# Later times in an instruction planner for attention weight parts, transposed keys and loaded queries

## The chip, the cores and the metric

The kernel runs on one core of a Trainium2 chip. The core has a matrix engine (TensorE, in the profile PE, with PEld for its weight loads), a vector engine (VectorE, DVE), a scalar engine (ScalarE, ACT), GpSimd (POOL) and SyncE (SP), which here issues DMAs. Each engine works through its own list of instructions in the order in which the program wrote them, and waits by semaphores for others. The metric is the device time of one execution in microseconds, smaller is better.

## The reference

Block-sparse attention for 4 batches of 8 heads, 768 positions and head size 64 is followed by a bilinear feed-forward network on the 3072 rows of its output:

```python
scores = scale * np.matmul(q, k.transpose(0, 1, 3, 2))
mask = np.abs(blk_i - blk_j) <= 1              # blocks of 32 positions, 24 of them
mask = mask | (blk_i == 0) | (blk_j == 0) | (blk_i == n_blocks - 1) | (blk_j == n_blocks - 1)
# and three sampled key blocks for each query block
attn = softmax(np.where(mask, scores, -1000000000.0))
x = (attn @ v).transpose(0, 2, 1, 3).reshape(3072, 512)
return ((x @ w_a) * (x @ w_b)) @ w_out         # 512 -> 1536 -> 512
```

## The kernel before

All products run in float16 with each operand split in a high and a low part, so that most products are made three times.

**Attention** works in units: one unit is one block of 32 query rows of one batch, 24 blocks in 4 batches, 96 units. A sparse unit (88 of them) gathers eight key blocks (POOL copies from the transposed keys `keysT` to `KG`) and eight value blocks (SP DMAs to `VG`); PE makes the scores `s` (L1024, L923); DVE takes the maximum `low` (L1039, L1042); ACT makes the exponentials `sm` (L1049); ACT or DVE write the high part of the weights and DVE the low part into a buffer `hl` (`in_parts`, L941, L944, L948); a DMA transpose turns `hl` into `pt` (L1074); PE multiplies `pt` with the values to `av` (L967); ACT and DVE split that into `xT` (L1233, L1236). The first and last block of each batch are dense: four pieces each, with their transposes at L1188. There are three buffers `hl` and three `pt`. The first eight units turn their weights on PE instead (L1101). In the text a unit is named by its number in the order of work, so `hl32` is the buffer contents of unit 32.

**Chunks.** Eight units make a chunk of 256 rows. For each chunk ACT issues the loads of its queries `q` in two halves (L691), reads them for a bound (L701), scales them (L706), DVE makes the low part (L708), and SP copies both to the other half of the partitions. **Feed-forward** takes a chunk's `xT` in twelve pieces: 24 matmuls `ab` (L1265), ACT and DVE make the product `a` and its parts `gh` and `gl` (L1282, L1285, L1294, L1297), six matmuls `o` (L1325 to L1327). A piece needs the whole chunk's `xT`. In the first 230 us DVE and ACT also turn the raw weights into parts (L768 to L816).

**The order** of every engine's list comes from a planner that runs when the program is built (`Plan`, L131). Each piece of work is a generator: it yields a `Way` (an engine, a duration in ns, what to issue), an `Event` it must wait for, or a number of ns by which it sleeps. The planner always issues the piece that can begin first by its own clock; ranks break ties and weigh on DVE and SP. A `Ring` gives out buffers: `take` waits until the one that is a ring's length back was freed, at the time its `fire` was given. For a DMA the planner reckons its own landing time (`issue`, L156). Times in the plan decide the order alone; on the chip the semaphores decide when an instruction starts. The names that matter here are `gone`, the event by which a buffer `hl` comes free (L1077, L1191), `done` and `k_ready` in `keys` (L524, L525), and the load in `queries` (L693).

Of the kernel before, what the change touches and what calls it, by code (L numbers as in the profile page):

```python
# [52 lines left out]

LATE_PT, LATE_VG, LATE_AV, LATE_G = 2500, 2500, 1500, 700
LATE_S = 1000
DMA_AHEAD = 1750
X_HIGH, X_UNITS = 600, 16

# [190 lines left out]
def kernel(  # L249
# [94 lines left out]
    k_ready = [Event(NG) for _ in range(B)]  # L344
# [143 lines left out]
    def keys(b, g):  # L488
        yield from gate(first_of[b] - GATE_KV)
        raw, freed = yield from raw_tile(b, g, 0)  # L490
        yield load_way(1000, lambda: nc.scalar.dma_start(raw, k[b, g]))
        if g + 1 < NG:
            plan.start(keys(b, g + 1), first_of[b] - LEAD_K)
        elif b > 0:
            plan.start(values(b, 0), first_of[b] - LEAD_V)
        t = raw.rearrange("p (t d) -> p t d", d=D)
        done = yield from take("ks", KS_BUFS)
        ks = work.tile([P, 2 * NT, P], F16, tag="ks", name=f"ks{b}_{g}", bufs=KS_BUFS)
        at = at_k + b * NG + g
        s = scale[:, at : at + 1]  # L500
        yield act(1020, lambda: nc.scalar.activation(
            ks[:, :, :D], t, AF.Abs, accum_out=bound[:, at : at + 1]
        ))
        end = yield from set_scale(slice(at, at + 1), FLOOR_QK)
        k_scale[b].fire(end)
        yield act(930, lambda: nc.scalar.activation(ks[:, :, :D], t, AF.Copy, scale=s))
        end = yield dve(1070, lambda: nc.vector.scalar_tensor_tensor(
            ks[:, :, D:], t, s, ks[:, :, :D], ALU.mult, ALU.subtract
        ))
        freed.fire(end)  # L510
        if b == 0:
            ends = Event(2)
            for h in range(2):
                plan.start(turn_keys(g, h, ks, ends, done), first_of[b] - LEAD_K, end)
            return
        if b == 1:
            yield w_freed
        if b >= 2:
            yield k_free[b - 2]
        end = yield sp(1700, 2200, lambda: nc.sync.dma_start_transpose(  # L520
            keysT[b % 2][:, 2 * g : 2 * g + 2, :].rearrange("p h (t s) -> p (h t) s", s=P),
            ks.rearrange("p t d -> p (t d)"),
        ))
        done.fire(end)  # L524
        k_ready[b].fire(end)  # L525

    def load_eye():
        end = yield load_way(100, lambda: nc.scalar.dma_start(eye, c_eye))
# [152 lines left out]
    def queries(cc):  # L681

        b, c = chunks[cc]
        u0 = order[b, c * PER]
        yield from gate(u0 - GATE_Q)
        freed = yield from take("rq", 1)
        t = work.tile([P, H, CH], F32, tag="rq", name=f"q{cc}", bufs=1)

        def load():
            for hs in (slice(0, H // 2), slice(H // 2, H)):  # L690
                nc.scalar.dma_start(t[:D, hs], q[b, c][:, hs])  # L691

        yield [Way("LOAD", 950, load, 1400, 1)]  # L693
        if cc + 1 < NC:
            b1, c1 = chunks[cc + 1]
            plan.start(queries(cc + 1), order[b1, c1 * PER] - LEAD_Q)
        at = at_q + cc
        q_used[cc] = yield from take("QT", QT_BUFS)
        QT[cc] = work.tile([P, 2, H, CH], F16, tag="QT", name=f"QT{cc}", bufs=QT_BUFS)
        high, low_ = QT[cc][:D, 0], QT[cc][:D, 1]  # L700
        yield act(2080, lambda: nc.scalar.activation(  # L701
            high, t[:D], AF.Abs, accum_out=bound[:D, at : at + 1]
        ))
        yield from set_scale(slice(at, at + 1), FLOOR_QK)
        s = scale[:D, at : at + 1]
        end = yield act(1890, lambda: nc.scalar.activation(high, t[:D], AF.Copy, scale=s))  # L706
        plan.start(turn_queries(cc, 0), u0 - LEAD_Q, end)
        end = yield dve(2350, lambda: nc.vector.scalar_tensor_tensor(  # L708
            low_, t[:D], s, high, ALU.mult, ALU.subtract
        ))  # L710
        freed.fire(end)
        plan.start(turn_queries(cc, 1), u0 - LEAD_Q, end)
        yield k_scale[b]

        def factor():

            for i in range(2):
                ps = slice(i * 64, (i + 1) * 64)
                nc.vector.tensor_scalar(
                    cq[ps, cc, :],  # L720
                    rscale[ps, at_k + b * NG : at_k + (b + 1) * NG].rearrange(
                        "p (a i) -> p a i", i=2
                    )[:, :, i],
                    rscale[ps, at : at + 1], float(D) ** -0.5, ALU.mult, ALU.mult,
                )

        end = yield dve(520, factor)
        q_ready[cc].fire(end)
# [278 lines left out]
    def attend(b, i):  # L1007
# [27 lines left out]
        t = yield pe(850, all_scores)  # L1035
# [35 lines left out]
        if n < TURNED:  # L1071
            yield from turn_weights(n, hl, pt, gone)
        else:
            t = yield sp(1300, 1500, lambda: nc.sync.dma_start_transpose(  # L1074
                pt, hl.rearrange("p a h k -> p (a h k)")
            ))
            gone.fire(t)  # L1077
            yield LATE_PT
        yield vg_ready[b, i, 0]
        yield from before(b, i)  # L1080
# [42 lines left out]
    def attend_quad(b, i, hq, ends):  # L1123
        n = order[b, i]
        cc = chunk_at[b, i // PER]
        kt = keysT[b % 2]
        at = n % LATE
        if hq > 0:
            yield quad_sent[b, i]
        reads, banks = [], []  # L1130
        for x in range(2):
            reads.append((yield from take("s", 2)))
            banks.append(psum.tile([P, HALF], F32, tag="s", name=f"s{n}_{hq}{x}", bufs=2))

        def half_scores(x):
            scores(
                banks[x], cc, i, hq, lambda h: kt[:, h, x * HALF : (x + 1) * HALF], True
            )

        for x in range(2):  # L1140
            t = yield pe(450, lambda x=x: half_scores(x))
        if hq == 0:
            quad_sent[b, i].fire(t - HOP)
        else:
            k_free[b].fire(t)
            next_unit(b, i, t - HOP)
        for x in range(2):
            yield dve(530, lambda x=x: nc.vector.tensor_reduce(
                low[:, at, hq, x : x + 1], banks[x], axis=mybir.AxisListType.X, op=ALU.max,
                negate=True,  # L1150
            ))
        m1 = low[:, at, hq, 0:1]
        yield dve(270, lambda: nc.vector.tensor_scalar(
            m1, m1, low[:, at, hq, 1:2], cq[:, cc, hq : hq + 1], ALU.min, ALU.mult
        ))
        sms, freed = [], []
        mine = yield from turn("sm", b, i, hq)
        for x in range(2):
            freed.append((yield from take("sm", SM_BUFS)))
            if x == 1:  # L1160
                mine.fire(0)
            sms.append(work.tile([P, HALF], F32, tag="sm", name=f"sm{n}_{hq}{x}", bufs=SM_BUFS))
            t = yield act(860, lambda x=x: nc.scalar.activation(
                sms[x], banks[x], AF.Exp, bias=m1, scale=cq[:, cc, hq : hq + 1],
                accum_out=den[:, at, hq, x : x + 1],
            ))
            reads[x].fire(t + LATE_S)
        d1 = den[:, at, hq, 0:1]
        d2 = den[:, at, hq, 1:2]
        yield dve(212, lambda: nc.vector.tensor_scalar(d1, d1, d2, EPS, ALU.add, ALU.add))  # L1170
        yield dve(150, lambda: nc.vector.tensor_scalar(
            d1, d1, float(2.0 ** -14), None, ALU.mult
        ))
        yield dve(160, lambda: nc.vector.reciprocal(d1, d1))
        mine = yield from turn("hl", b, i, hq)
        mine_pt = yield from turn("pt", b, i, hq)
        for x in range(2):
            gone = yield from take("hl", HL_BUFS)
            if x == 1:
                mine.fire(0)  # L1180
            hl = work.tile([P, 2, HALF], F16, tag="hl", name=f"hl{n}_{hq}{x}", bufs=HL_BUFS)
            t = yield from in_parts(sms[x], hl[:, 0], hl[:, 1], d1, HALF, False)
            freed[x].fire(t)
            kept = yield from take("pt", PT_BUFS)
            if x == 1:
                mine_pt.fire(0)
            pt = work.tile([P, 6, P], F16, tag="pt", name=f"pt{n}_{hq}{x}", bufs=PT_BUFS)
            t = yield sp(1100, 1130, lambda hl=hl, pt=pt: nc.sync.dma_start_transpose(  # L1188
                pt, hl.rearrange("p a k -> p (a k)")
            ))  # L1190
            gone.fire(t)  # L1191
            plan.start(all_values(b, i, hq, x, pt, kept), n, t + LATE_PT)

    def all_values(b, i, hq, x, pt, kept):
# [261 lines left out]
```

## Time and profile before

| | us |
|---|---|
| median of 3 runs | 874.8 |
| lowest and highest of them | 874.49, 878.71 |
| the profiled execution's own time | 871.27 |
| its span, from the first to the last instruction | 869.5 |
| PE busy in the span | 759.1 |
| DVE, ACT, POOL busy | 590.8, 501.3, 191.7 |

Busy time counts an instruction from its start to its end; waiting counts as idle. An instruction that waits holds back everything behind it on its engine. PE's ends are modelled, since matmuls overlap.

### The profile page before, as it was taken

How to read it: one execution, taken by the hardware profiler on the slowest of the kernel's cores; microseconds unless marked ns; L12 is line 12 of the kernel's file. 1: busy time of each engine (PE TensorE's matmuls, PEld its weight loads, DVE VectorE, ACT ScalarE, POOL GpSimd, SP SyncE). 2: the span in 40 equal slices, each digit the busy share in tenths (PEclk: the TensorE clock that was granted, in tenths of full speed). 3: DMA queues.
4: the chain of work that ended last, by engine and by line, in shares of the span. 5: the costliest groups of instructions: out<-in, count | busy, mean ns of one | idle time of the engine just before them, and what ended most of it. 6: DMA issues, size and time to landing. Idle time of an engine off the chain costs nothing.

```text
span 869.5 us, 24163 instructions
## 1 busy us (share of the span) xinstructions
PE 759.1 (87%) x9136; PEld 561.9 (65%) x9136; DVE 590.8 (68%) x1609; ACT 501.3 (58%) x1191; POOL 191.7 (22%) x428
## 2 busy tenths in 40 slices
PE   2246367599999979999999999999999999999998
PEld 1134245377767757766776667677777677777775
DVE  4979988999788666766576696766677776432222
ACT  6579787866766464774355586644656554332222
POOL 0743253200034232330032242200342310000000
PEclk9996689999999999999999999999999999999999
DMA  8766798795967479896586899767966766610000
GB/s 244 211 182 201 223 228 188 179 246 128 243 172 183 118 155 215 194 176 178 134 166 170 162 209 239 160 152 172 168 143 161 144 138 159 142 44 1 25 2 25
DMA packets 195151, 138.74 MB, mean 160 GB/s; under 512 B 138073, under 2 KB 162650, under 8 KB 195034
## 3 DMA queue, kind: packets, MB, share of 16 engines
q1 hardware_dynamic: 183104, 99.40, 52.3%
q10 hardware_dynamic: 11930, 37.79, 14.4%
q8 instruction: 72, 1.18, 0.6%
q14 instruction: 45, 0.37, 0.1%
HBM read 86.28 MB, written 12.58 MB: 114 GB/s over the span
## 4 chain that ended last, share of the span: by engine, by line
PE 47%; DVE 18%; DMA 18%; ACT 10%; issue 4%; SPq 2%; ACTq 1%; POOL 0%; POOLq 0%; DVEq 0%
PE ab L1265 25%; DMA pt<-hl 6%; PE av L967 5%; PE o L1325 5%; DMA q<-in_q_dram 5%; PE o L1327 4%; PE o L1326 4%; PE s L923 3%; DVE hl L948 2%; DMA VG<-vd 2%; DMA stage<-in_k_dram 2%; DVE QT L708 2%; DVE xT L1236 2%; ACT sm L1049 1%; ACT QT L706 1%
## 5 line engine op out<-in xcount | busy, mean ns | idle before, releaser
L1265 PE MATMUL ab<-xT,wab 128*128 128x256 f16 x3456 | 401.4, 273 | 6.0 <-DVE xT L1236 3.2
L1265 PEld LDWEIGHTS <-wab 128*128 128x128 f16 x3456 | 334.4, 98 | 68.5 <-issue 13.8
L1285 DVE SCALAR_TENSOR_TENSOR a<-a,to_g,ab 128x256 f32<-128x256 f32 x144 | 68.6, 477 | 104.8 <-ACT a L1282 103.7
L1282 ACT ACTIVATE a<-ab,w 128x256 f32<-128x256 f32 x144 | 67.3, 467 | 112.0 <-PE ab L1265 109.6
L1049 ACT ACTIVATE sm<-s,low,cq 128x256 f32<-128x256 f32 x176 | 97.7, 557 | 50.0 <-DVE low L1042 28.2
L948 DVE SCALAR_TENSOR_TENSOR hl<-sm,den,hl 128x256 f16<-128x256 f32 (+1 forms) x208 | 104.8, 512 | 27.7 <-ACT hl L941 25.5
L627 POOL COPY KG<-keysT 128x384 int32<-128x384 int32 x88 | 58.7, 667 | 283.5 <-PE s L923 251.4
L967 PEld LDWEIGHTS <-VG 128*128 128x128 f16 x2688 | 97.9, 100 | 29.3 <-issue 14.7
L1325 PE MATMUL o<-woh,gh 128*128 128x512 f16 x288 | 109.8, 381 | 7.9 <-ACT gh L1294 7.9
L967 PE MATMUL av<-pt,VG 128*128 128x64 f16 x2688 | 104.3, 196 | 11.0 <-DMA VG<-vd 7.4
L1327 PE MATMUL o<-wos,gl 128*128 128x512 f16 x288 | 109.3, 380 | 3.1 <-DVE gl L1297 2.6
L632 POOL COPY KG<-keysT 128x128 int32 x264 | 103.5, 428 | 36.7 <-POOL KG L627 26.3
L1326 PE MATMUL o<-wol,gh 128*128 128x512 f16 x288 | 109.2, 379 | 0.0
L1294 ACT ACTIVATE gh<-a 128x256 f16<-128x256 f32 x144 | 59.4, 413 | 60.6 <-DVE a L1285 55.8
L1297 DVE SCALAR_TENSOR_TENSOR gl<-gh,a 128x256 f16<-128x256 f16 x144 | 63.2, 440 | 34.2 <-ACT gh L1294 33.4
L941 ACT ACTIVATE hl<-sm,den 128x256 f16<-128x256 f32 (+1 forms) x91 | 46.0, 517 | 38.6 <-DMA pt<-hl 27.8
L923 PE MATMUL s<-KG,QT 128*32 128x256 f16 x1408 | 60.1, 295 | 6.6 <-POOL KG L632 6.1
L1236 DVE SCALAR_TENSOR_TENSOR xT<-av,xT 64x256 f16<-64x256 f32 x96 | 40.3, 420 | 33.0 <-ACT xT L1233 31.6
L1039 DVE TENSOR_REDUCE low<-s 128x2 f32<-128x512 f32 x88 | 60.0, 682 | 1.7 <-PE s L923 1.1
L1024 PE MATMUL s<-mrows,ident 128*32 128x192 bf16 (+1 forms) x352 | 25.9, 284 | 37.2 <-ACT sm L1049 25.3
L944 DVE TENSOR_SCALAR hl<-sm,den 128x256 f16<-128x256 f32 (+1 forms) x117 | 42.5, 365 | 19.7 <-DMA pt<-hl 19.4
L1327 PEld LDWEIGHTS <-gl 128*128 128x128 f16 x288 | 28.1, 98 | 42.4 <-DVE gl L1297 10.6
(115 smaller groups left out, 776.9 us busy)
## 6 DMA issues: line engine op xcount, KB each, us to landing
VG<-vd SPq DMA_DIRECT2D x284, 64.0 KB, 2.0
VG<-vd SPq DMA_DIRECT2D x88, 192.0 KB, 3.0
VG<-vd SPq DMA_DIRECT2D x32, 384.0 KB, 3.5
q<-in_q_dram ACTq DMA_DIRECT2D x24, 256.0 KB, 5.7
QT<-QT SPq DMA_DIRECT2D x24, 256.0 KB, 3.8
vd<-vs SPq DMA_DIRECT2D x16, 384.0 KB, 3.3
out_dram<-ou SPq DMA_DIRECT2D x24, 256.0 KB, 2.4
stage<-in_k_dram ACTq DMA_DIRECT2D x12, 384.0 KB, 5.5
```

What stands on the lines that cost most here:

```text
L632: nc.gpsimd.tensor_copy(to[:, :, (5 + r) * w : (6 + r) * w], of[:, :, bass.ds(at, w)])
L923: mm(to[h * BLK : (h + 1) * BLK], q_block(cc, i, 4 * hq + h, a), rhs(4 * hq + h), start=(first and a == 0), stop=(a == 1), skip_group_chec ...
L948: t = yield dve(221 + n * 1.03, lambda: nc.vector.scalar_tensor_tensor(lo, sm, over, hi, ALU.mult, ALU.subtract))
L967: mm(av[:, g, i % 2, :], w, pt[:, y, cols], start=(i % 2 == 0 and g == 0 and first and n + m == 0), stop=(last and n == len(terms) - 1 and ...
L1049: t = yield act(750, lambda hq=hq: nc.scalar.activation(sm[:, hq], ps[:, hq], AF.Exp, bias=low[:, at, hq, 0:1], scale=cq[:, cc, hq : hq + ...
L1265: mm(ab[:, i, :], wab[:, f, i, part, kt, :], xc[:, kt, a, :], start=(i == 0 and kt == 0 and part + a == 0), stop=(kt == KT - 1 and a == 1) ...
L1282: yield act(470, lambda: nc.scalar.activation(a_sb, ab[:, 0, :], AF.Copy, scale=w3[:, f : f + 1]))
L1285: t = yield dve(420, lambda: nc.vector.scalar_tensor_tensor(a_sb, a_sb, to_g[:, n : n + 1], ab[:, 1, :], ALU.mult, ALU.mult))
L1297: t = yield dve(460, lambda: nc.vector.scalar_tensor_tensor(gl, gh, -G_LOW, a_sb, ALU.mult, ALU.add))
L1325: mm(po, gh[:, js], woh[:, f, :], start=(f == lo), stop=False)
L1326: mm(po, gh[:, js], wol[:, f, :], start=False, stop=False)
L1327: mm(po, gl[:, js], wos[:, f, :], start=False, stop=(f == hi - 1))
```

## The change

Three constants are added, and some of the planner's times move. A buffer `hl` is now reckoned free 2500 ns after the landing that the planner reckons for its transpose, where it was free at that landing. The buffer `ks` of a key part, and the transposed keys made from it, are reckoned free and ready 2500 ns later. A chunk's queries are reckoned loaded 2000 ns later. Nothing is computed in another way; buffers, tiles and DMAs are the same.

```diff
+LATE_HL, LATE_KS, LATE_Q = 2500, 2500, 2000
...
-        done.fire(end)
-        k_ready[b].fire(end)
+        done.fire(end + LATE_KS)
+        k_ready[b].fire(end + LATE_KS)
...
         yield [Way("LOAD", 950, load, 1400, 1)]
+        yield LATE_Q
...
-            gone.fire(t)
+            gone.fire(t + LATE_HL)
             yield LATE_PT
...
-            gone.fire(t)
+            gone.fire(t + LATE_HL)
             plan.start(all_values(b, i, hq, x, pt, kept), n, t + LATE_PT)
```

The change moves instructions on all five engines. Three places follow. The line numbers of the changed kernel are one or two higher; the number behind a name is the buffer's serial and can be passed over.

The first place is ACT's list around the load of the fourth chunk's queries (`q3`), while unit 20 waits for its exponentials (`sm20`). Before:

```order
L691 DMA q3_2220<-in_q_dram 64x1024 x2
L1282 ACTIVATE a0_5_2316<-ab0_5_2162,w3_99 128x256
L1233 ACTIVATE xT1_89<-av0_4_2104 64x4x64 x2
L801 ACTIVATE wab_73,bound_91<-w24_1887 128x512
L1294 ACTIVATE gh0_5_2400<-a0_5_2316 128x256
L801 ACTIVATE wab_73,bound_91<-w25_2071 128x512
L752 DMA keysT1_79<-in_moe_w_b_dram 128x1024
L701 ACTIVATE QT3_2357,bound_91<-q3_2220 64x2048
L1352 ACTIVATE ou12_1_2450<-o0_0_1_1741,to_out_104 128x512
L1049 ACTIVATE sm20_2496,den_98<-s20_2287,low_97,cq_96 128x256
L801 ACTIVATE woh_74,bound_91<-w26_2353 128x512
L1049 ACTIVATE sm20_2496,den_98<-s20_2287,low_97,cq_96 128x256
```

In the changed kernel:

```order
L692 DMA q3_2298<-in_q_dram 64x1024 x2
L1051 ACTIVATE sm20_2465,den_98<-s20_2337,low_97,cq_96 128x256 x2
L803 ACTIVATE woh_74,bound_91<-w26_2439 128x512
L808 ACTIVATE wab_73<-w24_1643,scale_94 128x512
L754 DMA stage_77<-in_moe_w_b_dram 128x1024
L1235 ACTIVATE xT1_89<-av0_6_2367 64x4x64 x2
L703 ACTIVATE QT3_2494,bound_91<-q3_2298 64x2048
```

The first reading of the queries (`QT3` from `q3`) moved behind both exponentials of `sm20`, and behind the row that writes the last part of the second chunk's `xT1` (from `av0_6`), which stood five rows below the last one shown of before.

The second place is DVE's list between the low parts of the weights of unit 12 and unit 13, in the stretch where raw weights are still turned into parts (`wab`, `w23`). Before, from the last row of `hl12` to the last of `hl13`:

```order
L948 SCALAR_TENSOR_TENSOR hl12_1631<-sm12_1563,den_98,hl12_1631 128x256
L948 SCALAR_TENSOR_TENSOR hl13_1738<-sm13_1588,den_98,hl13_1738 128x256
L1042 TENSOR_TENSOR low_97<-low_97,cq_96 128x2
L809 SCALAR_TENSOR_TENSOR wab_73<-wab_73,scale_94 128x512
L1285 SCALAR_TENSOR_TENSOR a0_1_1716<-a0_1_1716,to_g_103,ab0_1_1620 128x256
L1236 SCALAR_TENSOR_TENSOR xT1_89<-av0_0_1245,xT1_89 64x4x64 x2
L948 SCALAR_TENSOR_TENSOR hl13_1738<-sm13_1588,den_98,hl13_1738 128x256
```

In the changed kernel, where the last row of `hl12` stands five rows ahead of the first one here:

```order
L777 SCALAR_TENSOR_TENSOR wab_73<-keysT1_79,wab_73 128x1024
L1299 SCALAR_TENSOR_TENSOR gl0_2_1914<-gh0_2_1874,a0_2_1801 128x256
L1041 TENSOR_REDUCE low_97<-s16_1827 128x2
L837 RECIPROCAL scale_94<-rscale_95 128x3
L1056 TENSOR_SCALAR den_98<-den_98 128x2
L770 TENSOR_SCALAR w23_1490<-keysT1_79 128x512
L1059 RECIPROCAL den_98<-den_98 128x2
L1044 TENSOR_TENSOR low_97<-low_97,cq_96 128x2
L839 SCALAR_TENSOR_TENSOR w3_99<-rscale_95 128x1
L774 SCALAR_TENSOR_TENSOR w23_1490<-keysT1_79,w23_1490 128x512
L811 SCALAR_TENSOR_TENSOR wab_73<-wab_73,scale_94 128x512
L950 SCALAR_TENSOR_TENSOR hl13_1825<-sm13_1632,den_98,hl13_1825 128x256
```

Sixteen instructions now stand between the last write of `hl12` and the first DVE write of `hl13`, where there was none.

The third place is ACT's list at the program's start, from the first reading of the first chunk's queries (`QT0`) to their scaling. Before:

```order
L701 ACTIVATE QT0_130,bound_91<-q0_116 64x2048
L752 DMA stage_77<-in_moe_w_a_dram 128x1024
L506 ACTIVATE ks0_2_125<-wab_73,scale_94 128x12x64
L547 COPY keysT0_78<-kt0_1_150 128x768
L501 ACTIVATE ks0_3_169,bound_91<-wab_73 128x12x64
L419 DMA mrow_118<-in_sampled_blocks_dram 1x144
L423 DMA mbox_117<-in_sampled_blocks_dram 24x6
L426 DMA mbox_117<-c_blocks 24x29
L547 COPY keysT0_78<-kt1_1_176 128x768
L752 DMA stage_77<-in_moe_w_b_dram 128x1024
L706 ACTIVATE QT0_130<-q0_116,scale_94 64x2048
```

In the changed kernel:

```order
L703 ACTIVATE QT0_130,bound_91<-q0_116 64x2048
L502 ACTIVATE ks0_3_171,bound_91<-wab_73 128x12x64
L754 DMA stage_77<-in_moe_w_b_dram 128x1024
L548 COPY keysT0_78<-kt1_1_177 128x768
L570 ACTIVATE va0_0_191,bound_v_92<-wab_73 128x768
L754 DMA stage_77<-in_moe_w_out_dram 128x1024
L548 COPY keysT0_78<-kt2_0_194 128x768
L754 DMA keysT1_79<-in_moe_w_a_dram 128x1024
L570 ACTIVATE va0_3_212,bound_v_92<-wab_73 128x768
L570 ACTIVATE va0_1_239,bound_v_92<-wab_73 128x768
L507 ACTIVATE ks0_3_171<-wab_73,scale_94 128x12x64
L708 ACTIVATE QT0_130<-q0_116,scale_94 64x2048
```

The third key part (`ks0_2`) is now scaled ahead of the first reading, and the value pieces (`va0`) and the scaling of the fourth key part (`ks0_3`) ahead of the scaling of `QT0`.

## Rows read from the trace of the kernel before

**Rows 1.** The page, busy time of each engine, share of the span, instructions.
```profile
PE 759.1 (87%) x9136; PEld 561.9 (65%) x9136; DVE 590.8 (68%) x1609; ACT 501.3 (58%) x1191; POOL 191.7 (22%) x428
```

**Rows 2.** Five stretches of the span: length, busy time by engine, granted clock, DMA.
```profile
core 0: us, PE busy (x) PEld busy (x) DVE busy (x) ACT busy (x) POOL busy (x), PEclk, DMA share, GB/s
0.00:60.00 60.00, 15.50 (x170) 10.86 (x170) 41.23 (x104) 37.24 (x70) 23.86 (x43) 1.00 0.76 220
60.00:175.00 115.00, 71.43 (x1046) 51.60 (x1047) 105.87 (x274) 94.89 (x225) 41.31 (x73) 0.84 0.81 199
175.00:400.00 225.00, 215.72 (x2561) 159.91 (x2559) 172.63 (x480) 142.85 (x342) 52.39 (x124) 1.00 0.78 186
400.00:760.00 360.00, 350.92 (x4537) 261.41 (x4536) 243.45 (x692) 198.98 (x496) 73.76 (x188) 1.00 0.74 163
760.00:869.50 109.50, 105.55 (x828) 78.16 (x826) 27.64 (x63) 27.29 (x60) 0.35 (x1) 1.00 0.05 19
```

**Rows 3.** Four stretches inside those, same columns.
```profile
300.00:350.00 50.00, 43.77 (x592) 32.09 (x591) 33.05 (x99) 28.12 (x69) 13.84 (x33) 1.00 0.82 181
450.00:550.00 100.00, 94.39 (x1253) 69.01 (x1251) 75.79 (x221) 64.98 (x155) 29.64 (x78) 1.00 0.88 193
575.00:625.00 50.00, 50.00 (x668) 38.15 (x666) 31.40 (x87) 24.93 (x63) 5.49 (x14) 1.00 0.69 152
650.00:725.00 75.00, 71.89 (x1032) 53.14 (x1031) 55.54 (x168) 44.53 (x120) 17.97 (x47) 1.00 0.68 152
```

**Rows 4.** Waits in 60 to 175 us: total us, times, longest.
```profile
PE s L1024 <- ACT sm L1049: 14.1, 6, 4.6
...
ACT QT L701 <- DMA q<-in_q_dram: 5.6, 2, 3.0
...
ACT hl L941 <- DMA pt<-hl: 3.2, 1, 3.2
```

**Rows 5.** Waits in 175 to 400 us.
```profile
ACT hl L941 <- DMA pt<-hl: 9.2, 4, 4.4
...
DVE hl L944 <- DMA pt<-hl: 5.8, 3, 3.3
...
ACT QT L701 <- DMA q<-in_q_dram: 3.3, 2, 2.2
```

**Rows 6.** Waits in 400 to 760 us.
```profile
ACT hl L941 <- DMA pt<-hl: 15.3, 9, 3.7
DVE hl L944 <- DMA pt<-hl: 13.5, 7, 5.2
POOL KG L627 <- DMA keysT<-ks: 12.7, 1, 12.7
...
ACT QT L701 <- DMA q<-in_q_dram: 9.5, 4, 3.5
```

**Rows 7.** DMA issues: count, KB of each, median us from issue to landing.
```profile
q<-in_q_dram ACTq DMA_DIRECT2D x24, 256.0 KB, 5.7
...
pt<-hl SPq DMA_TRANSPOSE x112, 4.0
```

**Rows 8.** Timeline of ACT, 156 to 172 us: start, us, idle before.
```profile
163.56 1.91 ACT L701 ACTIVATE QT<-q 64x2048 f16<-64x2048 f32 x1 [2.61 <-DMA q<-in_q_dram]
...
166.17 0.56 ACT L1049 ACTIVATE sm<-s,low,cq 128x256 f32<-128x256 f32 x1
...
167.33 0.56 ACT L1049 ACTIVATE sm<-s,low,cq 128x256 f32<-128x256 f32 x1
```

**Rows 9.** Timeline of PE, 160 to 176 us.
```profile
168.03 0.62 PE L1024 MATMUL s<-mrows,ident 128*32 128x512 bf16 x4 [4.60 <-ACT sm L1049]
...
171.75 0.38 PE L1265 MATMUL ab<-xT,wab 128*128 128x256 f16 x2 [0.85 <-ACT xT L1233]
```

**Rows 10.** Timeline at the start, ACT and PE.
```profile
13.15 1.91 ACT L701 ACTIVATE QT<-q 64x2048 f16<-64x2048 f32 x1 [2.91 <-DMA q<-in_q_dram]
...
32.29 1.04 PE L923 MATMUL s<-KG,QT 128*32 128x256 f16 x16 [4.75 <-POOL KG L632]
```

## The prediction

> **What bounds the kernel now.** I read the page's busy times first, then the same by stage, then the waits by stage, then the timeline at the longest wait of PE that a moved row touches. PE is busy 759.1 us of the span, far ahead of DVE and ACT [rows 1]; its matmuls are the same after the change, so what can be won or lost is PE's idle time. The reader is to see where that lies [rows 2]. In the first 60 us PE is idle for 44.5 us: loads and key parts come first. From 60 to 175 us it is idle for 115 - 71.43 = 43.6 us, while DVE is busy 105.87 of 115 us with weights and attention together: a stretch set mostly by DVE's list. From 175 to 760 us PE is idle for only 9.28 + 9.08 = 18.4 us. The rest is feed-forward alone with nothing else in the queues, and its order does not change.
>
> Those 18.4 us are lumped. Three stretches, 300 to 350, 450 to 550 and 650 to 725 us, hold 6.23 + 5.61 + 3.11 = 14.95 us, and 575 to 625 us holds none [rows 3]. From 175 us on ACT and DVE stand still at the head of their lists for DMAs that the plan held to be done: 24.5 us for a buffer `hl` on ACT (13 times), 19.3 us on DVE (10 times), 12.8 us for queries (6 times), 56.6 us in all, 29 times [rows 5, 6]. POOL once waits 12.7 us for transposed keys [rows 6], but POOL is busy 22% of the span and its gathers run ahead of the scores. A load of queries lands 5.7 us after its issue in the median and a transpose of `hl` 4.0 us [rows 7]; the plan's own sums (lines 156 to 170) give some 3.8 and 4.0 us on a free queue, so the first is short by about the 2 us that the change adds, and the second is right in the middle and short only for the late ones.
>
> **The change part by part.** No instruction is added; only the order and a few choices between ACT and DVE move, so each cost is a wait.
>
> Queries, late chunks. Between a load's issue and its first reading ACT had 31 instructions in the eight loads after 175 us, and has 57 in the new order (counted in both orders). That is 26 / 8 = 3.25 more per load, at ACT's mean of 501.3 / 1191 = 0.42 us [rows 1] about 1.4 us more cover, against 12.8 / 6 = 2.1 us per wait. So about two thirds, 8.5 us of ACT's waiting, go.
>
> Buffers `hl`. The order shows less here than the constants promise. In units from 20 on, the fewest DVE instructions between the last write of a buffer's old contents and the first of its new rise from 7 to 11, and the cases under 12 fall from 4 to 2 (counted). I take half of the 43.8 us of these waits; bounds are none of it and all of it. What is postponed has slack behind it as long as `pt` is the scarcer buffer, since a written `hl` waits for a free `pt` before its transpose can start.
>
> PE, 175 to 760 us. 8.5 + 21.9 = 30.4 of 56.6 us of waits gone is 54%. Of PE's idle time I put the 15 us of the three stretches to these waits, since the stretch without idle time has hardly any; 54% of it is 8 us. Against that I set 2 us for pieces that the margins push late elsewhere. So -6 us, between -15 (all of the lumped idle) and +4 (nothing goes, and the 2 us double).
>
> 60 to 175 us. The first place shown from the order is the clearest single gain. ACT sat 2.61 us at the first reading of `QT3`, read for 1.91 us, and only then made both exponentials of unit 20, starting at 166.17 and 167.33 us [rows 8]; PE stood 4.60 us for them until 168.03 us, since the scores of unit 22 need unit 20's bank, and 0.85 us later for the last part of `xT1` [rows 9]. It is the longest of the six waits of that kind in the stretch [rows 4]. In the new order both exponentials and that part of `xT1` stand ahead of the reading, so none of it waits for the load. I count 4.5 of the 5.45 us. The second place works the other way: sixteen DVE instructions before `hl13`, at DVE's mean of 590.8 / 1609 = 0.37 us [rows 1], are 5.9 us. Much of it is made up by unit 15; and the last DVE write of chunk 1's `xT` has two instructions fewer ahead of it than before (counted), among those now behind it the 64x2048 low part of `QT3`. I charge 1.5 us, bounds 0 and 5.9. Sum -3.
>
> Start. ACT waited 2.91 us for the first queries with a key part behind them; that part now goes first. The scaling of `QT0` comes later in exchange. The first scores waited last for POOL's gather at 32.29 us [rows 10], which needs the fourth key part, not the queries. I take 0, from -2 to +3.
>
> Key parts. 0: POOL's waits are covered by its own idle time; if that cover failed, 12.7 us of POOL waiting would stand ahead of one batch's first scores, while PE still has feed-forward pieces.
>
> Sum: -6 - 3 = -9 us on the profiled execution's 871.27, so 862.3. The median of the runs is 874.8, 3.5 above it, so I forecast 865.8, say 866.
>
> The Trainium skill speaks against the two larger terms. First: the page "DMA: Bandwidth & Descriptors", section "Anatomy of one DMA", puts a DMA at a nearly constant 2.0 us plus bytes over 436 GB/s (fitted on GpSimd's path). Two halves of 256 KB would then be down some 3.3 us after the issue (an estimate from that page), the plan would already be right, and the margins would only shift work: the sum would be 0. The median of 5.7 us [rows 7] and the waits disagree. Second: "Perfetto Trace Analysis", section "Identifying the Most-Contended Engine", says that matmul busy time misjudges how full PE is and that weight-load busy time tells it better. By that measure 175 to 400 us (159.91 of 225, 71%) is as full as the feed-forward end (78.16 of 109.5, 71%) [rows 2], and nothing is left there to gain. But attention's small matmuls load weights oftener, so the two shares are not of one mix.
>
> **The rivals.**
>
> The waits only move: the postponed write is itself what PE would wait for next, or drift between plan and chip eats the margins. For it: the `hl` distances hardly grow, and most of the 56.6 us cost PE nothing even now. Against it: the `QT3` place. Time 874.8, within 871 and 879.
>
> Slower: DVE's list from 100 to 175 us. The margin makes the planner fill DVE with weight pieces ahead of `hl11` to `hl15`. DVE is 92% busy there [rows 2], so it can't be made up by speed; if those parts, not a free `pt`, are what the transposes wait for, chunk 1's `xT` is late by up to 5.9 us and its first product starts after 171.75 us [rows 9] instead of before. PE has only chunk 0's first six pieces to fill with. That decides from the point where the 5.9 us exceed what `QT3` gives back (5.45 us) and what is won later. With no late gain: 874.8 + 5.9 = 881; with 3 us of it, 878.
>
> Larger gain: all the lumped idle (-15) and the `QT3` place (-4.5) without loss, 855; a likely size is 858.
>
> **How the numbers follow.** Forecast 0.49 (its own range 861 to 871), waits only move 0.22, slower 0.17, larger gain 0.12. A measurement of this kernel can tell about 0.5% from no change, so faster means under 870.4 and slower over 879.2. Faster: most of the forecast (0.45), the larger gain (0.12) and the edge of the second case (0.05), 0.62. Slower: most of the slower case (0.13) and the edge of the second (0.02), 0.15. The rest, 0.23, is no change. The range leaves out about one in ten at each end: the far half of the larger gain below 856, and the far part of the slower case above 879.
>
> **What would show it.** After 175 us the waits of ACT and DVE for `hl` and queries should fall from 56.6 to about 26 us, and PE's idle time there from 18.4 to about 12. PE's 4.60 us wait for the exponentials before unit 22's scores should be gone, and chunk 1's first product should start near 168 to 170 us. The waits of PE for `pt` or `VG` should not grow by more than 2 us. It is wrong if chunk 1's first product starts later than 172 us, if PE's idle time after 175 us is unchanged although the waits fell, or if the waits are as long as before.

## The result, and the profile after

The changed kernel takes 864.0 us in the median of four runs (858.84 to 877.41), the kernel before beside it 876.34 (874.49 to 878.71): a ratio of 0.986, 95% interval 0.981 to 0.991. When both were run again beside the experiments, the ratio was 0.990 (0.984 to 0.995). It is faster by 1.0 to 1.4%. The ratios leave out executions that took over 1.5% longer than the fastest of their kernel; the medians hold all. The profiled execution took 866.09 us, 5.2 less than the one of before. Line numbers in the changed kernel are one or two higher.

The busy line of the page, and the first four of the five stretches in [rows 2] (length, busy time of PE, PEld, DVE, ACT and POOL, granted clock, DMA share, GB/s):

```profile
PE 764.5 (88%) x9136; PEld 566.9 (66%) x9136; DVE 587.1 (68%) x1601; ACT 507.1 (59%) x1199; POOL 180.7 (21%) x428
```

```profile
0.00:60.00 60.00, 20.61 (x248) 14.52 (x248) 47.74 (x123) 43.45 (x86) 27.02 (x49) 0.99 0.75 235
60.00:175.00 115.00, 76.57 (x1076) 57.27 (x1074) 107.19 (x284) 94.23 (x223) 35.68 (x67) 0.75 0.94 222
175.00:400.00 225.00, 217.78 (x2499) 160.02 (x2497) 165.58 (x459) 140.38 (x329) 45.90 (x123) 0.97 0.74 174
400.00:760.00 360.00, 349.52 (x4537) 260.93 (x4535) 240.72 (x680) 203.06 (x505) 71.71 (x188) 1.00 0.72 161
```

The number of instructions beside PE's busy time tells more than the time. Ahead of 60 us PE issues 248 matmuls where it issued 170, and from 60 to 175 us 1076 for 1046: the work is ahead early. From 175 to 760 us PE is idle for (225 - 217.78) + (360 - 349.52) = 17.7 us, where it was 18.4 [rows 2].

Yet the waits that the change aims at are gone. From 175 to 400 us ACT and DVE wait nowhere for `hl` or for queries; from 400 to 760 us the rows that answer to [rows 6] are these (total us, times, longest):

```profile
ACT hl L943 <- DMA pt<-hl: 4.9, 4, 2.2
DVE hl L946 <- DMA pt<-hl: 3.3, 4, 1.6
...
ACT QT L703 <- DMA q<-in_q_dram: 2.7, 4, 1.2
```

That is 10.9 us where there were 56.6 [rows 5, 6]. So 46 us of ACT's and DVE's waiting went, and PE's idle time behind 175 us stayed. ACT and DVE did not stand idle for less either: from 175 to 760 us the two were idle for 243.2 + 168.9 us before [rows 2] and for 241.6 + 178.7 us after. The waiting moved to other causes.

The place of `QT3` came out as read from the order, though PE's wait there did not go entirely. On ACT both exponentials of unit 20 and the last part of `xT1` now stand ahead of the reading, which no longer waits; on PE the scores of unit 22 wait 1.80 us instead of 4.60, and the second chunk's first product starts 10.7 us earlier than in [rows 9]. ACT's timeline, then PE's:

```profile
154.37 0.56 ACT L1051 ACTIVATE sm<-s,low,cq 128x256 f32<-128x256 f32 x1 [1.19 <-DVE hl L950]
...
154.93 0.55 ACT L1051 ACTIVATE sm<-s,low,cq 128x256 f32<-128x256 f32 x1
...
161.00 1.91 ACT L703 ACTIVATE QT<-q 64x2048 f16<-64x2048 f32 x1
```

```profile
155.62 0.62 PE L1026 MATMUL s<-mrows,ident 128*32 128x512 bf16 x4 [1.80 <-ACT sm L1051]
...
161.02 0.58 PE L1267 MATMUL ab<-xT,wab 128*128 128x256 f16 x2 [0.86 <-ACT xT L1235]
```

**The start** holds what the prediction had put at 0. The first product with values (`av` of unit 0) starts at 52.75 us, before at 60.22. Most of these 7.5 us are a stand on ACT; the rest was not followed. ACT's timeline before:

```profile
47.56 0.48 ACTq L691 DMA_DIRECT2D q<-in_q_dram  x1
...
53.58 0.47 ACTq L691 DMA_DIRECT2D q<-in_q_dram  x1
54.10 0.51 ACT L941 ACTIVATE hl<-sm,den 128x256 f16<-128x256 f32 x1 [5.56 <-DMA VG<-vd]
```

The two halves of the second chunk's queries are issued one behind the other in ACT's list, and 6 us apart in time: ACT stands for 5.56 us at the second issue, with `hl` of the next unit behind it. DVE waits 4.61 us for that `hl`, and then PE, on whose timeline this row stands:

```profile
54.66 0.91 PE L1101 MATMUL pt_t<-eye,hl 128*128 128x128 f16 x6 [5.15 <-ACT hl L941]
```

What ACT waits for shows in the chain of waits before, from 44 to 61 us (start, us, what):

```profile
49.24 4.32 DMA VG<-vd
53.56 0.02 issue
53.58 0.47 ACTq L691
54.05 0.05 issue
54.10 0.51 ACT hl L941
```

A load of values, issued by SP at 49.24 us, has to land before ACT may issue a load of queries that has nothing to do with it. The program's lists say why. Each of its 688 DMAs reports to one of eight counters, and in the lists each is issued only after its engine has waited for all earlier ones on its counter. ACT's list before and after, with the counters waited for:

```
63 L691 DMA q1_497<-in_q_dram 64x1024 [waits DMAHW4_49]
64 L691 DMA q1_497<-in_q_dram 64x1024 [waits DMAHW7_49]
...
64 L692 DMA q1_498<-in_q_dram 64x1024 [waits DMAHW3_49]
65 L692 DMA q1_498<-in_q_dram 64x1024 [waits DMAHW5_49]
```

On counter 7 that second half stands, before, behind a part of `VG0` (L664), which is the load in the chain above: it landed at 53.56 us, and the half was issued at 53.58. After, the halves stand on counters 3 and 5, behind a write of `vd0` and a load of raw weights that were issued earlier. ACT's timeline after:

```profile
45.42 0.51 ACT L943 ACTIVATE hl<-sm,den 128x256 f16<-128x256 f32 x1 [0.42 <-DVE den L1059]
45.53 0.48 ACTq L692 DMA_DIRECT2D q<-in_q_dram  x1
...
46.06 0.61 ACTq L692 DMA_DIRECT2D q<-in_q_dram  x1
```

**Given back.** Of the lead of 10.7 us the end keeps 5.2. In both kernels 7940 matmuls are left at the second chunk's first product. From there to the end, before and after:

```profile
171.75:869.50 697.75, 674.43 (x7940) 501.34 (x7939) 446.93 (x1240) 372.35 (x904) 126.64 (x313) 1.00 0.65 148
```

```profile
161.02:864.30 703.28, 679.27 (x7940) 504.72 (x7939) 445.41 (x1233) 382.85 (x918) 119.61 (x314) 0.99 0.63 146
```

PE is idle for 23.3 us before and 24.0 after, and busy 4.8 us longer with the same number of matmuls. So what is given back is nearly all in slower matmuls, with a granted clock that is 1.00 throughout before and 0.99 after. One place is at 219 us. ACT's timeline, PE's, and three stretches:

```profile
219.02 0.84 ACT L502 ACTIVATE ks<-stage 128x768 f16<-128x768 f32 x1 [3.21 <-DMA stage<-in_k_dram]
...
219.86 0.40 ACT L1296 ACTIVATE gh<-a 128x256 f16<-128x256 f32 x1
```

```profile
220.32 0.61 PE L1327 MATMUL o<-woh,gh 128*128 128x512 f16 x1 [3.12 <-ACT gh L1296]
```

```profile
210.00:220.00 10.00, 7.19 (x73) 5.67 (x71) 5.45 (x25) 4.64 (x11) 1.05 (x3) 0.97 0.98 213
220.00:230.00 10.00, 9.68 (x78) 6.39 (x79) 6.54 (x13) 6.13 (x12) 0.36 (x1) 0.69 0.86 191
...
318.50:325.00 6.50, 5.22 (x40) 3.66 (x38) 3.75 (x17) 6.06 (x11) 1.77 (x6) 0.50 0.95 283
```

ACT waits for a raw key load, which has no margin, with `gh` behind it. PE stands 3.12 us, and behind that gap the granted clock is 0.69 in the mean of the stretch, a mixture of its upper level (2.4 GHz) and its lower one (1.2 GHz, 0.50 here): a matmul `o` takes 0.61 us where it took 0.38 just before. At 318.5 us the clock is at the lower level once more, behind a gap of 1.87 us on PE.

### The profile page after: what moved, and what is told of

Its sections match the earlier page's. It is cut to its first block, busy times and chain, and to the rows that moved or that the text cites. A ratio compares the mean times of both kernels' runs of the same rounds, so it can differ in the third digit from the quotient of the medians.

```text
span 864.3 us, 24142 instructions
## 1 busy us (share of the span) xinstructions
PE 764.5 (88%) x9136; PEld 566.9 (66%) x9136; DVE 587.1 (68%) x1601; ACT 507.1 (59%) x1199; POOL 180.7 (21%) x428
## 3 DMA queue, kind: packets, MB, share of 16 engines
q1 hardware_dynamic: 183104, 99.40, 51.9%
## 4 chain that ended last, share of the span: by engine, by line
PE 49%; DVE 16%; DMA 12%; ACT 10%; issue 9%; SPq 1%; POOL 1%; ACTq 0%; POOLq 0%; DVEq 0%
PE ab L1267 26%; PE av L969 5%; PE o L1327 5%; PE o L1329 4%; PE o L1328 4%; PE s L925 3%; DVE hl L950 3%; DMA pt<-hl 3%; DMA stage<-in_k_dram 2%; ACT sm L1051 2%; DMA VG<-vd 2%; DVE low L1041 2%; DMA q<-in_q_dram 2%; ACT xT L1235 1%; DVE xT L1238 1%
## 5 line engine op out<-in xcount | busy, mean ns | idle before, releaser
L1267 PE MATMUL ab<-xT,wab 128*128 128x256 f16 x3456 | 407.6, 275 | 9.9 <-DVE a L1287 7.4
L969 PE MATMUL av<-pt,VG 128*128 128x64 f16 x2688 | 106.1, 197 | 16.3 <-DMA pt<-hl 8.0
L633 POOL COPY KG<-keysT 128x128 int32 x264 | 92.4, 387 | 41.2 <-POOL KG L628 22.9
L1296 ACT ACTIVATE gh<-a 128x256 f16<-128x256 f32 x144 | 59.6, 415 | 56.4 <-DVE a L1287 52.2
L925 PE MATMUL s<-KG,QT 128*32 128x256 f16 x1408 | 59.8, 294 | 10.5 <-POOL KG L633 8.0
L1235 ACT ACTIVATE xT<-av 64x256 f16<-64x256 f32 x96 | 36.2, 377 | 45.6 <-PE av L969 44.4
L925 PEld LDWEIGHTS <-QT 128*32 128x32 f16 x1664 | 43.9, 102 | 22.8 <-issue 12.6
L943 ACT ACTIVATE hl<-sm,den 128x256 f16<-128x256 f32 (+1 forms) x97 | 49.0, 520 | 14.6 <-DMA pt<-hl 4.9
```

The lines of the kernel that those rows point to most:

```text
L633: nc.gpsimd.tensor_copy(to[:, :, (5 + r) * w : (6 + r) * w], of[:, :, bass.ds(at, w)])
L925: mm(to[h * BLK : (h + 1) * BLK], q_block(cc, i, 4 * hq + h, a), rhs(4 * hq + h), start=(first and a == 0), stop=(a == 1), skip_group_chec ...
L969: mm(av[:, g, i % 2, :], w, pt[:, y, cols], start=(i % 2 == 0 and g == 0 and first and n + m == 0), stop=(last and n == len(terms) - 1 and ...
L1267: mm(ab[:, i, :], wab[:, f, i, part, kt, :], xc[:, kt, a, :], start=(i == 0 and kt == 0 and part + a == 0), stop=(kt == KT - 1 and a == 1) ...
```

## The experiments

Twelve runs, in three groups of four, each group on one chip. AV is the start of the first product with values and AB that of the second chunk's first product, both from PE's timeline of the profiled execution; "rest" is the time from AB to the start of the last six products `o`. The ratio is to the kernel before on the same chip. AV, AB and "rest" come from one execution of each kernel, and executions of one kernel differ: the profiled one of e6 is the fastest of its ten (860.47 to 877.02), that of e2 the fastest of its ten (867.32 to 880.76). The medians and ratios are the safer numbers.

| kernel | ratio (95%) | AV | AB | rest |
|---|---|---|---|---|
| before | 1 | 60.2 | 171.7 | 692.5 |
| e3_ks_only | 1.012 (1.005, 1.019) | 59.8 | 170.1 | 709.5 |
| e4_nudge | 0.996 (0.992, 1.001) | 60.9 | 168.4 | 699.6 |
| e9_late | 1.008 (1.004, 1.011) | 59.6 | 168.2 | 703.4 |
| e2_hl_only | 0.998 (0.994, 1.003) | 60.6 | 167.2 | 693.1 |
| e6_q_rest | 0.996 (0.992, 1.000) | 59.5 | 163.5 | 690.0 |
| e1_q_only | 0.990 (0.982, 0.997) | 53.0 | 165.7 | 697.7 |
| e5_q_first | 1.017 (1.008, 1.025) | 51.2 | 166.5 | 705.9 |
| changed | 0.986 (0.981, 0.991) | 52.8 | 161.0 | 698.1 |
| e11_after_again (the same) | 0.990 (0.984, 0.995) | 51.5 | 156.0 | 696.7 |
| e7_early | 0.993 (0.989, 0.997) | 52.6 | 156.7 | 699.4 |
| e8_raw | 0.984 (0.981, 0.988) | 52.6 | 158.8 | 692.8 |
| e12_raw_again (the same) | 0.989 (0.984, 0.993) | 53.3 | 159.3 | 693.8 |
| e10_after_nudge | 0.984 (0.979, 0.989) | 51.9 | 159.8 | 693.3 |

**One margin at a time.** The first three leave two of the three constants at 0; the fourth is the kernel before with a margin for `g` that has nothing to do with the change, to see what any new order does.

```diff
-LATE_HL, LATE_KS, LATE_Q = 2500, 2500, 2000
+LATE_HL, LATE_KS, LATE_Q = 0, 0, 2000      # e1_q_only
+LATE_HL, LATE_KS, LATE_Q = 2500, 0, 0      # e2_hl_only
+LATE_HL, LATE_KS, LATE_Q = 0, 2500, 0      # e3_ks_only
```
```diff
-LATE_PT, LATE_VG, LATE_AV, LATE_G = 2500, 2500, 1500, 700
+LATE_PT, LATE_VG, LATE_AV, LATE_G = 2500, 2500, 1500, 720   # e4_nudge
```

> Only the queries' margin of 2000 ns; the two others 0. Theory A (the gain is the queries' margin before 175 us, where the first product of the second chunk came 10.7 us sooner): that product starts near 161 us again and the time is 864 to 868. Theory B (the freed waits for hl, 44 us of ACT and DVE time, pay): only the queries' part, 870 to 874, since hl waits stay at some 40 us. Theory C (any other order scatters by several us): no reason to be near either, 860 to 885.

> Only the margin of the buffers hl; PE's order is that of before for its first 61 blocks. Theory A: waits for hl after 175 us fall below 15 us, but the first product of the second chunk stays near 171 us and the time is 872 to 878. Theory B: 866 to 870. Theory C: anywhere from 865 to 885.

> Only the key parts' margin; PE's order is that of before for its first 116 blocks, past 200 us. Theories A and B: 874 to 879, no change beyond 0.5%. Theory C: a change of 4 us or more either way is as likely as none.

> The kernel before with a constant of no concern here nudged (the margin of the parts gh and gl 720 ns for 700): another order from PE's 208th block on, some 365 us, with no margin added. Theories A and B: 874 to 879. Theory C: a change of 4 us or more either way.

Queries alone gave 869.54 us (before 874.98), `hl` alone 875.63, keys alone 886.39, the nudge 872.98, which is no change that can be told. With `hl` alone the `hl` waits after 175 us fell from 43.8 to 10.7 us, and PE's idle time from 175 to 760 us only from 18.4 to 16.9 us. Theory B, that the freed waits pay, is refuted with its 866 to 870 us; the interval leaves room for a gain of 0.6%. With queries alone these waits rose to 59.5 us, and it is faster. Theory A is not met in its numbers either: AB came at 165.7 us where 161 was expected, and the time 1.5 us above its range. The keys alone left the 874 to 879 us of both theories. The three do not add up: -1.0, -0.2 and +1.2% against -1.4% together.

**The queries' margin, split.**

```diff
-        yield LATE_Q
+        yield LATE_Q if cc == 0 else 0      # e5_q_first
+        yield 0 if cc == 0 else LATE_Q      # e6_q_rest
```
(with the two other constants at 0)

> The margin of 2000 ns stands only behind the load of the first chunk's queries; all later queries, hl and the keys are reckoned as before. Theory S (the start): the new order of the first 60 us is what gives the lead; the first product with values (AV 0) comes 6 to 8 us earlier than the 60.2 us of before and the second chunk's first ab product 4 to 7 us earlier than 171.7; time 867 to 871. Theory T (the QT3 place): the start's lead is eaten by the stretch that DVE's list sets until 175 us, and the ab product starts within 2 us of before; time 872 to 877. Theory C (any new order scatters by several us behind 175 us): the lead at 175 us and the end have little to do with each other, either theory may show its place at 160 to 175 us and end anywhere from 868 to 880.

> The complement: the margin of 2000 ns stands behind all query loads but the first chunk's. Theory S: AV 0 within 1 us of before (60.2), the second chunk's first ab product at most 2 us earlier, time 872 to 877. Theory T: that product 4 to 5 us earlier (near 167) because the exponentials of unit 20 no longer stand behind the reading of the fourth chunk's queries, and PE's wait of 4.6 us at 163 to 168 us is gone; time 868 to 871. Theory C: as for the run before, 868 to 880 whatever stands at 175 us.

They took 883.33 and 868.77 us (before 873.71). The column AV splits all fourteen traces without exception: with the margin for the first chunk's queries 51.2 to 53.3 us, without it 59.5 to 60.9. ACT's timeline of e6 shows the stand of before again, that of e5 does not:

```profile
46.15 0.48 ACTq L692 DMA_DIRECT2D q<-in_q_dram  x1
52.27 0.50 ACTq L692 DMA_DIRECT2D q<-in_q_dram  x1
52.82 0.51 ACT L943 ACTIVATE hl<-sm,den 128x256 f16<-128x256 f32 x1 [5.42 <-DMA VG<-vd]
```

```profile
44.26 0.48 ACTq L692 DMA_DIRECT2D q<-in_q_dram  x1
44.79 0.61 ACTq L692 DMA_DIRECT2D q<-in_q_dram  x1
```

All six traces without the margin have it (5.16 to 5.70 us of ACT's time), and none of the eight with it. But the gain does not last by itself: e5 is 9 us early at AV, 3 to 5 us at AB, and has the worst ratio of all, with the longest "rest" but one. Theory S has the place right and the time wrong. In these two executions both parts of the margin move AB, e6 clearly (163.5 us) and e5 by less than executions of one order differ (see below), so neither theory alone holds.

**Early or late.** e7 keeps the margins for the first four chunks' queries and for `hl` up to unit 22, without any for keys; e9 has the rest of them.

```diff
-        yield LATE_Q
+        yield LATE_Q if cc <= 3 else 0      # e7_early; e9_late: cc > 3
...
-            gone.fire(t + LATE_HL)
+            gone.fire(t + (LATE_HL if n < 23 else 0))   # e7_early; e9_late: n > 22
```

> All margins as in the changed kernel for the first four chunks' queries and for hl of the units up to 22, none later and none for keys; PE's order is the changed kernel's for the first 116 blocks, past 200 us. Theory E (the gain is made ahead of 175 us, the late margins do nothing for PE): second chunk's first ab product at 161 us as in the changed kernel, waits of ACT and DVE for hl and queries after 175 us back above 35 us, and still 861 to 867 in time. Theory L (the late margins keep the lead): the lead of 9 us at 175 us melts, time 869 to 875. Theory C: the end lies anywhere within 859 to 873.

> The margins for hl and queries only from unit 23 and the fifth chunk on, and for the keys as in the changed kernel; before that the plan is the kernel before's (PE's order is the same for 116 blocks, past 200 us). Theory E (the gain is made ahead of 175 us): the second chunk's first ab product within 3 us of before's 171.7; waits of ACT and DVE for hl and queries after 175 us fall to 10 to 20 us as in the changed kernel, and still no gain: 871 to 878. Theory L (the late margins gain by themselves): 864 to 869 and PE's idle time in 175 to 760 us at 12 us or less. Theory C (late order scatters): anything within 865 to 885.

This pair tells most. e7 took 865.08 us (before 873.71) although its waits for `hl` and queries after 175 us are back at 51.4 us. e9 took 880.84 (before 873.82) although these rows are all that is left of them from 175 to 760 us (DVE's, then ACT's):

```profile
DVE hl L946 <- DMA pt<-hl: 2.8, 4, 1.6
```

```profile
ACT hl L943 <- DMA pt<-hl: 1.8, 2, 1.0
ACT sm L1051 <- DMA pt<-hl: 1.3, 1, 1.3
ACT QT L703 <- DMA q<-in_q_dram: 0.3, 1, 0.3
```

Theory E's times were 861 to 867 us for e7, which it met, and 871 to 878 for e9, which it did not (AB, 3.5 us ahead of before, is also just outside); e9 has the keys' margin too, whose cost follows below. PE's idle time from 175 to 760 us is 19.5 us in e7 and 21.7 in e9.

The gain is made ahead of AB. Kernels with the early order of before (before, e3, e4, e9) reach AB at 168.2 to 171.7 us, mean 169.6; those with the changed kernel's early order (the last six of the table) at 156.0 to 161.0, mean 158.6. So the early order is worth 11 us there, against 3.5 and 5 us by which executions of one early order differ. The four kernels with the changed early order have ratios of 0.984 to 0.993, the three that have the early order of before 0.996 to 1.012. An early AB alone is not enough, as e5 shows.

e9 and e3 lose a good part at one place, which comes from the keys' margin on the early order of before. ACT's and PE's timeline of e9:

```profile
241.29 0.84 ACT L570 ACTIVATE va<-stage 128x768 f16<-128x768 f32 x1 [3.42 <-DMA keysT<-ks]
...
248.55 0.84 ACT L570 ACTIVATE va<-stage 128x768 f16<-128x768 f32 x1 [6.32 <-DMA stage<-in_v_dram]
...
249.39 0.65 ACT L1165 ACTIVATE sm<-s,low,cq 128x384 f32<-128x384 f32 x1
```

```profile
248.70 1.12 PE L969 MATMUL av<-pt,VG 128*128 128x64 f16 x18 [5.90 <-DMA pt<-hl]
```

ACT reads raw values ahead of the exponentials of a dense unit, and the DMAs come late: from 205 to 260 us the four value loads take 9.1 us in the median and the four transposes of keys 8.0 us, before 4.9 and 5.2. PE is idle for 5.90 us here, 6.79 us in e3. In the kernel before the third reading also stands ahead and waits only 2.81 us, and PE does not wait for it. In the changed kernel the first of these exponentials stands ahead of the third reading, and PE does not wait there.

**A margin for the raw loads, and a nudge.**

```diff
         yield load_way(1000, lambda: nc.scalar.dma_start(raw, k[b, g]))
+        yield LATE_RAW if b else 0          # e8_raw, e12_raw_again: 2500; the same for v
```
```diff
-LATE_PT, LATE_VG, LATE_AV, LATE_G = 2500, 2500, 1500, 700
+LATE_PT, LATE_VG, LATE_AV, LATE_G = 2500, 2500, 1500, 720   # e10_after_nudge, on the changed kernel
```

> The changed kernel with one more margin: the raw key and value loads of batches 1 to 3 are reckoned landed 2500 ns later. Theory R (the lead was partly given back at 219 us, where ACT stood 3.2 us for a raw key load with gh behind it, PE stood 3.1 us and its granted clock fell): that wait is gone, the granted clock of 220 to 230 us is back at its upper level, the lead at 225 us is 3 to 5 us larger than the changed kernel's and the time 857 to 862. Rival: the same piece waits elsewhere, or the order behind it scatters: 862 to 872.

> The changed kernel with a number that has nothing to do with it moved a little (the margin of the products g, 720 for 700 ns). PE's order is the changed kernel's for 94 blocks, to about 190 us, and another one behind it. Theory E: lead at 175 us as in the changed kernel (7 to 13 us) and 860 to 868. Theory C: the same lead at 175 us, and an end anywhere in 855 to 880; a difference of more than 4 us from the changed kernel in the same call is put to the order behind 190 us alone.

> The changed kernel once more, beside the others of this call on one chip, to compare directly: 862 to 867; its second chunk's first ab product at 157 to 164 us (161.0 in its first profile), which gives how much one execution's lead differs from another's.

> The changed kernel with the margin of 2500 ns for raw key and value loads once more, beside the changed kernel on one chip. Theory R: 4 to 6 us below the changed kernel. Theory C: a lucky order or a lucky chip; within 2 us of the changed kernel.

In e8 ACT's wait at 219 us fell to 1.99 us, PE's was gone, the granted clock from 220 to 230 us was 1.00, and e8 took 858.95 us, as theory R had it. But on one chip with the changed kernel it took 867.61, and that 867.12 (ratios 0.989 and 0.990), against theory R's 4 to 6 us: no gain that can be told. The nudge took 859.34 on the same chip, just under theory E's 860; its interval overlaps that of the changed kernel, so nothing is shown to beat it. The changed kernel's second run, e11, is just outside what was expected in time and in AB. The two pairs of one kernel have a "rest" within 1.4 and 1.0 us of each other, while it goes from 690.0 to 709.5 us over the kernels. That suggests that the order sets what happens behind 175 us, and it is not shown: four executions stand for it, and those of e12 lie up to 18 us apart. That margins alone make no good order is shown by e3, e5 and e9, which are slower.

## Why the prediction was right in the sum and wrong in its terms

**The number.** 866 was forecast; 864.0 and 867.1 are the medians. The split was -6 late, -3 in the middle and 0 at the start; it came out as about -11 by the second chunk's first product, of which 5 were given back behind it. That the sum fits is luck: the late gain did not come, and the gain ahead of it was 8 us larger than forecast.

**The premise.** The matmuls are the same, so the prediction let only PE's idle time change. That failed: over the span PE's idle time fell by 10.6 us (869.5 - 759.1 = 110.4 before, 864.3 - 764.5 = 99.8 after), and its busy time with the same 9136 matmuls rose by 5.4, with a lower granted clock from 60 to 175 us (0.75 for 0.84) and from 175 to 400 us (0.97 for 1.00). The sum had no term for the clock.

**175 to 760 us, -6.** This step failed. Its first half, that waits would fall, was too small (to about 26 us; it was 10.9). Its second, that 15 us of PE's idle time belonged to those waits because both lay in the same stretches, was wrong: PE's idle time is 17.7 us with the waits gone, and over the same 7940 matmuls it is 24.0 us for 23.3. e2 shows it without the other margins (waits for `hl` down by 33.1 us, PE's idle time by 1.5), e9 and e7 from both sides. The prediction had named this sign as one that would make it wrong, and in that term it does. Followed back to their releasers, PE's waits in the kernel before from 175 to 760 us were for `pt` only 1.8 us long in all, and the longest sum, 4.5 us, was for `gh`. No gain to PE from a shorter wait of ACT or DVE for a buffer is seen here. That the waits just moved is the rival that held in this stretch; the sum did not follow it, for the reason below.

**Start, 0 (from -2 to +3).** This step failed too. It looked at the first chunk's queries and at PE's gather wait at 32 us, and not at the 5.15 us for which PE stood at 54 us. The margin's effect there was not the one that it was made for: it moved which load shares a counter with which. What of it is left at AB can't be taken from one run: e5, with it alone, has AB 3.1 us ahead of the mean of the early order of before, e6, without it, 6.1.

**60 to 175 us, -3.** Right in its mechanism, too small in size. The place of `QT3` went as described, with 1.80 us of PE's 4.60 left. What the DVE list ahead of `hl13` cost, charged at 1.5 us and made into the slower rival, can't be told apart: AB came earlier, not later. How the rest of the 11 us divides between `hl` and queries stays open: alone they bring AB forward by 2.4 and 3.9 us against that mean, with the keys' together by 11. Even the 2.4 is not like for like, since e2 has started 20 matmuls fewer by AB (1177 for 1197).

**Key parts, 0.** Not shown on the changed kernel. On the early order of before the keys' margin costs 1.2% (e3), through ACT's readings of raw values, a path that the prediction did not look at.

**Open.** Why PE is idle for 13.8 us between 400 and 650 us in e5, where it is 5.9 before, why the granted clock drops at 318 us in the changed kernel, and why executions of one kernel lie up to 18 us apart (855.45 to 873.87 in e12), was not found.

## What to carry to other kernels

Before the idle time of the bounding engine is put to another engine's waits, follow each gap of the bounding engine back to its releaser; that both lie in the same stretch is no evidence. Look at every DMA that an engine issues as a place where it can stand: the issue itself may wait for an unrelated transfer on a shared counter. And where a planner sets the order, change a number that should not matter as well, and compare medians: here such a nudge moved the "rest" of one execution by 7 us with no change in the median that can be told, and one part of the change, the keys' margin, moved it by 17 us and the ratio to 1.012.

## What was not expected of the hardware

An issue of a load held ACT for 5.2 to 5.7 us in six traces, and the profile books that wait on the instruction behind it. A gap of 3.12 us on PE was followed by a granted clock of 0.69 over 10 us, and slower matmuls took 4.8 us of a lead of 10.7. Value loads of 384 KB took 9.1 us to land in e9 and 4.9 us before, beside four transposes of keys in both.
